# Leftover expert groups of 32 tokens, as four narrow fp32 products side by side inside the last large group's first layer

## The chip, the cores and the metric

The kernel runs on one core of one Trainium2 chip. The metric is device time in microseconds (us) of one execution. Three runs of the kernel before gave 670.18, 671.89 and 675.13 us; the median is 671.89 us.

## The reference, cut to what matters

Three layers follow each other. Attention with hash buckets (2 batches, 8 heads, 768 positions, 64 wide) gives 1536 rows of 512. A gated product without experts (`w1`, `w2`, `w3`, `w_out`) turns them into `x`, again 1536 x 512. A mixture of 8 experts ends the kernel, and the change is in it:

```python
def _moe2_ref(x, modality_id, w_gate, modality_bias, w1, w2):
    logits = x @ w_gate + modality_bias[modality_id]
    e_idx = np.argmax(logits, axis=1)
    ...                                   # probs, gate_w: the softmax weight of the chosen expert
    for e in range(E):
        mask = e_idx == e
        if not mask.any():
            continue
        h = np.maximum(x[mask] @ w1[e], 0.0)               # 512 -> 1024
        out[mask] = gate_w[mask, None] * (h @ w2[e])       # 1024 -> 512
    return out
```

Each token goes to one expert alone. With the inputs that the runs use, the argmax of the reference picks two experts only, one for 786 tokens and one for 750.

## The kernel before, in words

**Groups.** The tokens of one expert are cut into large groups of G = 256. What is left over (the count modulo 256) is another large group if it is more than 128, and otherwise a *leftover group* of 128 places (`half_group`, name "H"). For 786 tokens that is three large groups and 18 tokens in a leftover group, for 750 tokens three large groups (256, 256, 238). The program holds NFULL = 6 large groups and one leftover group in straight code (`static`), in that order; any further ones run in a loop at the end (`tc.For_i`), which runs no turn when there are none. Counts, thresholds (`cs[:, 16:28]`) and places (a column of 128 places per half of a large group, one column per leftover group, NCOL columns in all) are computed on the chip by VectorE (DVE), and the list of tokens of each column comes from 12 small products on TensorE (PE), `pv`.

**Products.** A large group is computed in three terms: each 32-bit operand is split into a rounded high part and the low rest (type fp32r), and high x high, high x low and low x high are summed (`TERMS`). `stage1` computes the first layer: for each of 8 blocks `f` of 128 hidden units, 12 products (4 chunks of the 512 inputs, 3 terms) of 128x128 weights with 256 tokens, then ScalarE (ACT) takes the ReLU as the high part and DVE the low part. `stage2` computes the second layer: for each of two halves of 128 tokens 24 products with 512 columns, then `put` scales by the gate and GpSimd (POOL) scatters the rows to `out`. A leftover group does the same with tokens as the stationary side: 24 products of 512 columns, 8 transposes, 24 products of 512 columns.

**Weights.** Each group loads its expert's two weight matrices anew, as 8 units of 512 KB (`load_raw`, issued by SyncE, SP, into a ring of 4 buffers). `split_raw` splits a unit: ACT copies the high part, DVE subtracts for the low part. The order is a list: `seq` gives the units in the order of the groups, `split_next` takes the next one, and calls `more_loads` for the load that may now use the buffer that has come free. `hook1` and `hook2` call `split_next` at fixed blocks of `stage1` and `stage2`, 8 times in a group, so that group j's hooks split the units of group j+1. `hook2` also issues the gathers (`gather`, POOL) of the group after next and the transposes (`trans`, PE) of the next one.

**Full 32-bit products.** Where both operands are plain fp32 (not fp32r) a product leaves two records in the trace. Four such products with a stationary side of 32 columns stand side by side (`tile_position=(0, 32*k)`, each writing its own 32 partitions of one PSUM tile) in several places of this kernel; two of them matter here. `logit_mm` (L708) has four of 384 columns, and `w34_gate` (L583) four of 128 columns:

```python
PE.matmul(lg_t[ch][k:k + 32, :], wgp[:, f, :], gf_t[ch, f4][:, f % 4, :], ..., tile_position=(0, k))       # L708
PE.matmul(pg[32 * c:32 * c + 32, :], wgs[:, c, :], wT[:, c, :], ..., tile_position=(0, 32 * c))            # L583
```

PSUM tiles: tag `ab` has 4 buffers, `t` has 2, `aw0` and `aw1` one each. The program's order on each engine is the order in which the code issues.

Of the kernel before, what the change touches and what calls it, by code (L numbers as in the profile page):

```python
# [20 lines left out]
P = 128  # L21
# [7 lines left out]
NFULL, MAXF, MAXH = 6, 9, 8  # L29
NCOL = 2 * MAXF + MAXH  # L30
# [43 lines left out]
def consts_array(proj):  # L74
# [17 lines left out]
    c[:, 16:28] = float(P) * np.arange(12)  # L92
# [78 lines left out]
def body(tc, qT, kT, vP, w1d, w2d, w3d, wod, mod, wgate, mbias, e1, e2, cst, out):  # L171
# [1006 lines left out]
    for i in range(2):  # L1178
        xg_t["F", 0, i] = r_xg([P, DM])
        POOL.memset(xg_t["F", 0, i], 0.0)  # L1180
    static = [("F", j) for j in range(NFULL)] + [("H", 0)]
    eregs = {
        (t, j): nc.values_load(
            egi[0:1, MAXF * (t == "H") + j:MAXF * (t == "H") + j + 1], engines=SPE, min_val=0, max_val=E - 1
# [5 lines left out]
    seq = [(j, m, k) for j in static for m in range(2) for k in range(4)]  # L1190
    lq = list(seq)
# [6 lines left out]
    def load_raw(j, m, k, e):  # L1198
        raw = r_er([P, 1024])
        SP.dma_start(raw if m == 0 else raw.rearrange("p (c f) -> p c f", c=2), unit_src(m, k, e))  # L1200
        eraw[j, m, k] = raw
# [90 lines left out]
    def cols(t, j):  # L1292
        if j[0] == "H":
            return [t[:, 2 * MAXF + j[1]:2 * MAXF + j[1] + 1]]
        return [t[:, 2 * j[1] + i:2 * j[1] + i + 1] for i in range(2)]

    def gather(j, idx, rows=NT):
        for i, ix in enumerate(idx):
            if (*j, i) not in xg_t:
                xg_t[*j, i] = r_xg([P, DM])  # L1300
            POOL.indirect_dma_start(
                out=xg_t[*j, i], out_offset=None, in_=x2d[0:rows, :],
# [62 lines left out]
    for span in gspan:  # L1365
        mem.give(span)

    r_eu.grow(2, 4 * 2 * 4096)
    r_h = ring("h", 2 * 8 * G, 2)
    r_o = ring("o", DM, 3)  # L1370
    r_hn = ring("hn", DF, 1)

    def trans(j):
        n = G if j[0] == "F" else P
        x = r_ex([P, 2, 4, n], F32R)
        for i in range(n // P):
# [34 lines left out]
    def stage2(j, gcol, scol, hook=None):  # L1411
        h = h_t.pop(j)
        w = wu.pop((j, 1)).rearrange("p x (c n) -> p x c n", c=8)
        for i in range(2):
# [7 lines left out]
            put(o, gcol[i], scol[i])  # L1422

    def put(o, gate_col, row_col, n=DM):
        ot = r_o([P, DM])
        ACT.activation(ot[:, 0:n], o[:, 0:n], AF.Copy, scale=gate_col)  # L1426
        if n < DM:
            DVE.tensor_scalar(ot[:, n:], o[:, n:], gate_col, None, ALU.mult)  # L1428
        POOL.indirect_dma_start(  # L1429
# [4 lines left out]
    def half_group(j, gcol, scol, hook=None):  # L1434
        hook = hook or (lambda n: None)
        x = x2_t.pop(j)
        w = wu.pop((j, 0)).rearrange("p x (c n) -> p x c n", c=4)
        hn = r_hn([P, DF])
        h = r_h([P, 2, 8, P], F32R)

        def htrans(n):
            t = ps("t", [P, 4, P], f"ht{j[0]}{j[1]}{n}")
            for c in range(4):
                PE.transpose(t[:, c, :], hn[:, n * 512 + c * P:n * 512 + c * P + P], ident)
            sl = slice(4 * n, 4 * n + 4)
            ACT.copy(h[:, 0, sl, :], t)
            DVE.tensor_sub(h[:, 1, sl, :], t, h[:, 0, sl, :].bitcast(F32))

        for n in range(2):
            o = ps("aw"[n], [P, 512], f"e1{j[0]}{j[1]}{n}")  # L1450
            for c in range(4):
                for i, (st, mv) in enumerate(TERMS):
                    PE.matmul(
                        o, x[:, st, c, :], w[:, mv, c, n * 512:n * 512 + 512],
                        start=(c == 0 and i == 0), stop=(c == 3 and i == 2),
                    )
                if n == 1 and c == 1:
                    htrans(0)
                hook(4 * n + c)
            ACT.activation(hn[:, n * 512:n * 512 + 512], o, AF.Relu)  # L1460
        w = wu.pop((j, 1)).rearrange("p x (c n) -> p x c n", c=8)
        o = ps("ab", [P, DM], f"e2{j[0]}{j[1]}")
        for f in range(8):
            for k, (st, mv) in enumerate(TERMS):
                PE.matmul(o, h[:, st, f, :], w[:, mv, f, :], start=(f == 0 and k == 0), stop=(f == 7 and k == 2))
            if f == 1:
                htrans(1)
            hook(8 + f)
        put(o, gcol[0], scol[0], DM // 2)
# [104 lines left out]
```

## Time and profile before

| | |
|---|---|
| three runs | 670.18, 671.89, 675.13 us |
| the profiled execution, its own time | 671.4 us |
| its span in the trace | 669.2 us |
| PE busy in the span | 640.7 us (96%) |
| DVE, ACT, POOL busy | 384.4, 318.5, 320.2 us |
| six large groups on PE | from 509.45 to 649.47 us of the span |
| the leftover group on PE, after them | from 649.31 to 661.34 us |
| from the last product to the end of the span | 7.9 us |

The times of the trace are microseconds from the start of the span. The profiled execution's own time is 2.2 us more than its span, and 0.5 us under the median of the runs.

### The profile page before, as it was taken

The page shows a single profiled execution, that of the slowest core. Times are in us where ns is not written, and L with a number is a line of the kernel's source. Part 1 is how long each engine was busy: PE and PEld are TensorE (multiplying, and loading weights), DVE is VectorE, ACT ScalarE, POOL GpSimd, SP SyncE. Part 2 cuts the span into 40 slices and gives each one's busy share as a digit, 9 for nine tenths or more (in the row PEclk, how much of TensorE's full clock was granted, in tenths as well). Part 3 has the DMA queues.
Part 4 walks back from the last instruction along what each step waited for, and adds up shares of the span by engine and source line. Part 5 has one row for each costly group of instructions (what it writes and reads, how often), then busy time and mean ns, then how long its engine had stood idle before and what let it go on. Part 6 is the DMA issues. An engine that isn't in the chain of part 4 may idle for free. (4 is left out here: it accounts for less than half of the span.)

```text
span 669.2 us, 10109 instructions
## 1 busy us (share of the span) xinstructions
PE 640.7 (96%) x3640; PEld 505.6 (76%) x3640; DVE 384.4 (57%) x573; ACT 318.5 (48%) x510; POOL 320.2 (48%) x291
## 2 busy tenths in 40 slices
PE   6998999999999998999999999999999999999995
PEld 2544666666666665687998988999889899889984
DVE  6798777667786999833531311211566775575551
ACT  7367575666556655753421220321134665565551
POOL 7598988686869777766341340421104222201110
PEclk9999999999999999999999999999999999999999
DMA  7747482654647474312302001000046896765630
GB/s 227 245 139 171 158 251 90 180 186 127 221 122 217 129 235 137 120 48 80 123 6 66 24 0 48 1 0 17 17 157 235 309 300 227 237 226 189 215 121 9
DMA packets 40662, 93.86 MB, mean 140 GB/s; under 512 B 6544, under 2 KB 11008, under 8 KB 40608
## 3 DMA queue, kind: packets, MB, share of 16 engines
q1 hardware_dynamic: 38528, 86.62, 41.9%
q0 software_dynamic: 2080, 6.56, 2.8%
q8 instruction: 30, 0.49, 0.3%
q14 instruction: 24, 0.20, 0.1%
HBM read 72.98 MB, written 12.94 MB: 128 GB/s over the span
## 5 line engine op out<-in xcount | busy, mean ns | idle before, releaser
L685 PE MATMUL ab<-x,w 128*128 128x384 f32 x512 | 135.3, 339 | 0.6 <-ACT ss L412 0.6
L385 POOL TENSOR_TENSOR acc<-acc,pt 128x770 f32<-128x770 f32 x64 | 119.9, 1873 | 21.6 <-ACT pt L380 19.9
L355 DVE TENSOR_REDUCE nm<-m 128x1 f32<-128x768 f32 x96 | 91.4, 955 | 49.6 <-PE m L347 49.2
L380 ACT ACTIVATE pt<-s 128x768 f32<-128x768 f32 x96 | 77.9, 811 | 72.0 <-PE s L379 69.8
L685 PEld LDWEIGHTS ab<-x,w 128*128 128x128 f32 x512 | 93.5, 188 | 5.8 <-issue 4.4
L379 PE MATMUL s<-q,k 128*128 128x384 f32 (+1 forms) x384 | 91.0, 359 | 4.0 <-ACT pt L380 3.8
L379 PEld LDWEIGHTS s<-q,k 128*128 128x128 f32 (+1 forms) x384 | 63.6, 189 | 38.7 <-issue 16.2
L697 POOL TENSOR_TENSOR g<-gf,g 128x384 fp32r<-128x384 f32 x32 | 32.9, 1029 | 119.5 <-ACT g L696 116.0
L685 PE MATMUL ab<-xlo,w 128*128 128x384 f32 x256 | 86.4, 338 | 0.0
L1217 DVE TENSOR_TENSOR eu<-er,eu 128x1024 fp32r<-128x1024 f32 x56 | 68.4, 1242 | 24.1 <-ACT eu L1216 22.6
L393 PE MATMUL a<-pt,v 128*64 128x385 f32 x384 | 74.5, 502 | 0.0
L1429 POOL DMA_INDIRECT out<-o,sidx x13 | 13.7, 1050 | 118.0 <-ACT o L1426 102.0
L1400 PEld LDWEIGHTS e1F<-ex,eu 128*128 128x128 f32 x576 | 69.2, 189 | 0.4
L1400 PE MATMUL e1F<-ex,eu 128*128 128x256 f32 x576 | 69.4, 281 | 0.0
L1419 PE MATMUL e2F<-eu,h 128*128 128x512 f32 x288 | 68.9, 395 | 0.0
L695 DVE TENSOR_TENSOR gf<-asb,ab 128x384 f32<-128x384 f32 x32 | 17.7, 553 | 84.0 <-PE ab L685 83.4
L1216 ACT CAST eu<-er 128x1024 fp32r<-128x1024 f32 x56 | 57.5, 1048 | 9.2 <-DMA er<-e 7.7
L1419 PEld LDWEIGHTS e2F<-eu,h 128*128 128x128 f32 x288 | 53.2, 188 | 11.4 <-DVE h L1406 0.3
L347 PE MATMUL m<-k,q 78*128 78x384 f32 x192 | 52.4, 355 | 5.2 <-DVE nm L355 2.7
L1024 PE MATMUL x2p<-w,g 128*128 128x512 f32 x240 | 57.4, 396 | 0.0
L1024 PEld LDWEIGHTS x2p<-w,g 128*128 128x128 f32 x240 | 44.8, 188 | 10.9 <-issue 0.6
L600 PE MATMUL w<-wo,w 128*128 128x512 f32 x192 | 49.0, 393 | 0.4 <-POOL w L495 0.4
(208 smaller groups left out, 863.0 us busy)
## 6 DMA issues: line engine op xcount, KB each, us to landing
er<-e SPq DMA_DIRECT2D x56, 512.0 KB
cr<-w3d SPq DMA_DIRECT2D x16, 512.0 KB
cr<-wod SPq DMA_DIRECT2D x8, 512.0 KB
cr<-w1d SPq DMA_DIRECT2D x8, 512.0 KB
wfd<-cT SPq DMA_DIRECT2D x16, 256.0 KB
cr<-w2d SPq DMA_DIRECT2D x8, 512.0 KB
st<-wfd SPq DMA_DIRECT2D x16, 256.0 KB
raw<-kT SPq DMA_DIRECT2D x8, 384.0 KB
```

What stands on the lines that cost most here:

```text
L347: PE.matmul(s[:, half, 0:HS], q[0:KROWS[hd], 0, qt * P:qt * P + P], k[0:KROWS[hd], 0, half * HS:half * HS + HS], start=True, stop=True,)
L355: DVE.tensor_reduce(nm[:, at:at + 1], s[:, :, 0:HS], AX.XY, ALU.max, negate=True)
L379: PE.matmul(s[:, hd, 0:HS], k[0:n, i, c * P:c * P + P], q[0:n, i, cl], start=(i == 0), stop=(i == 1))
L380: ACT.activation(pts[j % NP][:, :, 0:HS], s[:, :, 0:HS], AF.Exp, scale=SCALE)
L385: POOL.tensor_add(acc, pts[(j - 1) % NP] if c == 1 else acc, pts[j % NP])
L393: PE.matmul(a_t[p, half][64 * hd:64 * hd + 64, :], v[:, c, 64 * hd:64 * hd + 64], pts[j % NP][:, hd, :], start=(c == 0), stop=(c == QT - 1 ...
L685: PE.matmul(t, w12[j][:, st, c, fs], x[mv][:, c, :], start=(c == 0 and i == 0), stop=(c == 3 and i == 2))
L1024: PE.matmul(st["ps"], g_t[ch, f // 4][:, a, f % 4, i * P:i * P + P], w34[b][:, f, :], start=(f == 0 and k == 0), stop=(f == 7 and k == 2),)
L1216: ACT.copy(t[:, 0, sl], raw)
L1217: low = lambda: DVE.tensor_sub(t[:, 1, sl], raw, t[:, 0, sl].bitcast(F32))
L1400: PE.matmul(o[f], w[:, st, c, fs], x[:, mv, c, :], start=(c == 0 and i == 0), stop=(done and c == 3 and i == terms[-1]),)
L1419: PE.matmul(o, h[:, st, f, sl], w[:, mv, f, :], start=(f == 0 and k == 0), stop=(f == 7 and k == 2))
```

## The change: what it does, and the diff

A leftover group holds 32 places in place of 128; more than 32 tokens left over now make a large group. The one static leftover group is computed by `tiny_group` in four steps, which `hook1` issues after the blocks f = 0, 1, 2 and 3 of the last large group's `stage1`. Its products are full 32-bit ones of the loaded weights, without a split: the 32 tokens are the stationary side, and four products write four strips of 32 partitions. In the first layer a strip is a quarter of the 1024 hidden units (256 columns), in the second a quarter of the 512 outputs (128 columns). Its 8 weight units have buffers of their own (`tw`), and their loads stand one by one in the list after every fourth load of the large groups, from the 20th to the 48th. The hidden layer's buffer `h` of the large groups is one in place of two, and the last large group's last `put` is shared between ACT and DVE, as the leftover group's was.

```diff
-NFULL, MAXF, MAXH = 6, 9, 8
-NCOL = 2 * MAXF + MAXH
+NFULL, MAXF, MAXT = 6, 12, 8
+NCOL = 2 * MAXF + MAXT
+TINY_N = 32
...
-    c[:, 16:28] = float(P) * np.arange(12)
+    c[:, 16:28] = (G * np.arange(6)[:, None] + TINY_N * np.arange(2)[None, :]).reshape(12)
...
-    static = [("F", j) for j in range(NFULL)] + [("H", 0)]
+    static = [("F", j) for j in range(NFULL)] + [("T", 0)]
...
-    seq = [(j, m, k) for j in static for m in range(2) for k in range(4)]
-    lq = list(seq)
+    seq = [(j, m, k) for j in static[:NFULL] for m in range(2) for k in range(4)]
+    lq = []
+    for n, item in enumerate(seq):
+        lq.append(item)
+        if n >= 16 and n % 4 == 3:
+            lq.append((static[NFULL], (n - 19) // 16, (n - 19) // 4 % 4))
+    tw = []
...
-        raw = r_er([P, 1024])
+        if j[0] == "T":
+            raw = tw[m][k]
+        else:
+            raw = r_er([P, 1024])
...
                 load_raw(j, m, k, eregs[j])
+                while lq and lq[0][0][0] == "T":
+                    j, m, k = lq.pop(0)
+                    load_raw(j, m, k, eregs[j])
...
+    for n in ("lastx", "lastoh"):
+        rings[n].close()
...
-    r_h = ring("h", 2 * 8 * G, 2)
+    r_h = ring("h", 2 * 8 * G, 1)
     r_o = ring("o", DM, 3)
-    r_hn = ring("hn", DF, 1)
+    r_tx = ring("tx", 4 * TINY_N, 1)
+    r_hn = ring("hn", DF // 4, 1)
+    r_hT = ring("hT", DF // 4, 1)
+    tw += [[one(f"tw{m}{k}", [P, 1024]) for k in range(4)] for m in range(2)]
...
-            put(o, gcol[i], scol[i])
+            put(o, gcol[i], scol[i], DM // 2 if end and i else DM)
...
-    def half_group(j, gcol, scol, hook=None):
...
+    def tiny_group(j, gcol, scol):
+        n, st = TINY_N, {}
+
+        def transposed():
+            xg = xg_t.pop((*j, 0))
+            t = ps("t", [P, 4, n], f"et{j[0]}{j[1]}")
             for c in range(4):
+                PE.transpose(t[:, c, :], xg[0:n, c * P:c * P + P], ident[0:n, 0:n])
+            st["x"] = r_tx([P, 4, n])
+            ACT.copy(st["x"], t)
+
+        def layer1():
+            o = ps("t", [P, DF // 4], f"e1{j[0]}{j[1]}")
             for c in range(4):
+                for k in range(4):
+                    w = k * (DF // 4)
                     PE.matmul(
+                        o[n * k:n * k + n, :], st["x"][:, c, :], tw[0][c][:, w:w + DF // 4],
+                        start=(c == 0), stop=(c == 3), tile_position=(0, n * k),
                     )
+            st["h"] = r_hn([P, DF // 4])
+            ACT.activation(st["h"], o, AF.Relu)
+
+        def turned():
+            t = ps("t", [P, 2, P], f"ht{j[0]}{j[1]}")
+            for b in range(2):
+                PE.transpose(t[:, b, :], st["h"][:, b * P:b * P + P], ident)
+            st["hT"] = r_hT([P, 2, P])
+            ACT.copy(st["hT"], t)
+
+        def layer2():
+            o = ps("t", [P, P], f"e2{j[0]}{j[1]}")
+            for f in range(8):
+                k, b = divmod(f, 2)
+                for q in range(4):
+                    w = b * DM + q * P
+                    PE.matmul(
+                        o[n * q:n * q + n, :], st["hT"][:, b, n * k:n * k + n], tw[1][k][:, w:w + P],
+                        start=(f == 0), stop=(f == 7), tile_position=(0, n * q),
+                    )
+            raw, ot = r_o([P, DM]), r_o([P, DM])
+            for q in range(4):
+                DVE.tensor_copy(raw[0:n, q * P:q * P + P], o[n * q:n * q + n, :])
+            DVE.tensor_scalar(ot[0:n, :], raw[0:n, :], gcol[0], None, ALU.mult)
+            scatter(ot[0:n, :], scol[0])
+
+        return [transposed, layer1, turned, layer2]
 
     gather(static[1], cols(gidx, static[1]))
-    for n, j in enumerate(static):
+    tiny = tiny_group(static[NFULL], cols(inv[:, 1, :], static[NFULL]), cols(sidx, static[NFULL]))
+    for n, j in enumerate(static[:NFULL]):
         def hook1(f):
             if f % 2 == 1 or n == 0:
                 split_next()
+            if n == NFULL - 1 and f < 4:
+                tiny[f]()
...
```

The loop at the end is changed in the same way and is left out here.

On PE the end of the program reads as follows before; `e1F` and `e2F` are the two layers of the last large group, `etH`, `e1H`, `htH` and `e2H` the transposes and layers of the leftover group, with the output's shape and the number of products behind.

```order
L1400 MATMUL e1F_5980<-ex_5783,eu_5658 128x256 x12
L1419 MATMUL e2F_5999<-eu_5772,h_5861 128x512 x12
L1380 MATMUL etH_6016<-ident_70,xg_5798 128x128 x4
L1419 MATMUL e2F_5999<-eu_5772,h_5861 128x512 x12
L1419 MATMUL e2F_6042<-eu_5772,h_5861 128x512 x24
L1453 MATMUL e1H_6078<-eu_5892,ex_6015 128x512 x12
L1453 MATMUL e1H_6092<-eu_5892,ex_6015 128x512 x6
L1444 MATMUL htH_6099<-ident_70,hn_6076 128x128 x4
L1453 MATMUL e1H_6092<-eu_5892,ex_6015 128x512 x6
L1465 MATMUL e2H_6113<-eu_6006,h_6077 128x512 x6
L1444 MATMUL htH_6120<-ident_70,hn_6076 128x128 x4
L1465 MATMUL e2H_6113<-eu_6006,h_6077 128x512 x18
```

With the change the last large group's first layer is on PE (its blocks f = 0 to 4 are shown, with lines of the changed file; `etT`, `e1T`, `htT`, `e2T` are the steps of the leftover group):

```order
L1417 MATMUL e1F_5870<-ex_5797,eu_5673 128x256 x12
L1461 MATMUL etT_5885<-ident_70,xg_5812 128x32 x4
L1417 MATMUL e1F_5892<-ex_5797,eu_5673 128x256 x12
L1470 MATMUL e1T_5907<-tw_397_4650,tx_5890 32x256 x4
L1470 MATMUL e1T_5907<-tw_398_4651,tx_5890 32x256 x4
L1470 MATMUL e1T_5907<-tw_399_4652,tx_5890 32x256 x4
L1470 MATMUL e1T_5907<-tw_400_4653,tx_5890 32x256 x4
L1417 MATMUL e1F_5926<-ex_5797,eu_5673 128x256 x12
L1480 MATMUL htT_5941<-ident_70,hn_5924 128x128 x2
L1417 MATMUL e1F_5946<-ex_5797,eu_5673 128x256 x12
L1490 MATMUL e2T_5961<-tw_401_4654,hT_5944 32x128 x8
...
L1417 MATMUL e1F_6004<-ex_5797,eu_5673 128x256 x12
```

Three more rows of `e2T`, 8 products each, stand where the dots are. After block f = 7 come the 48 products of `e2F`, and nothing behind them.

On ACT the same stretch has, with the change, the ReLUs of the large group's blocks and the leftover group's copies between them; the four weight casts that stood there before are gone.

```order
L1422 ACTIVATE h_5869<-e1F_5870 128x256
L1463 COPY tx_5890<-etT_5885 128x128
L1422 ACTIVATE h_5869<-e1F_5892 128x256
L1475 ACTIVATE hn_5924<-e1T_5907 128x256
L1422 ACTIVATE h_5869<-e1F_5926 128x256
L1482 COPY hT_5944<-htT_5941 128x256
L1422 ACTIVATE h_5869<-e1F_5946 128x256
```

Each copy now stands right behind the ReLU of the block that PE computed just before the step.

## Rows read from the trace of the kernel before

**Rows 1.** The page: busy time by engine, and PE and its clock in 40 slices.
```profile
PE 640.7 (96%) x3640; PEld 505.6 (76%) x3640; DVE 384.4 (57%) x573; ACT 318.5 (48%) x510; POOL 320.2 (48%) x291
PE   6998999999999998999999999999999999999995
PEclk9999999999999999999999999999999999999999
```

**Rows 2.** Busy time by stretch, one per large group, then leftover group and tail.
```profile
core 0: us, PE busy (x) PEld busy (x) DVE busy (x) ACT busy (x) POOL busy (x), PEclk, DMA share, GB/s
509.90:532.60 22.70, 22.70 (x148) 20.36 (x147) 15.62 (x22) 14.32 (x23) 4.78 (x4) 1.00 0.83 300
532.60:556.00 23.40, 23.40 (x154) 21.20 (x153) 17.27 (x21) 14.70 (x22) 6.74 (x5) 1.00 0.90 287
556.00:579.50 23.50, 23.50 (x155) 21.43 (x154) 14.04 (x18) 13.06 (x20) 4.09 (x4) 1.00 0.71 229
...
626.60:649.50 22.90, 22.90 (x150) 20.88 (x149) 13.44 (x17) 12.56 (x19) 1.96 (x2) 1.00 0.47 147
649.50:661.40 11.90, 11.85 (x56) 9.43 (x55) 1.38 (x2) 3.06 (x5) 0.98 (x1) 1.00 0.05 21
661.40:669.30 7.90, 0.00 (x0) 0.00 (x0) 0.48 (x1) 0.47 (x1) 0.98 (x1) 0.83 0.03 8
```

**Rows 3.** Who waited for whom from 475 us on: total us, times, longest.
```profile
ACT eu L1216 <- DMA er<-e: 7.7, 7, 1.9
...
PE xb L1340 <- DMA xg<-x2d,gidx: 0.9, 1, 0.9
```

**Rows 4.** Timeline of PE, last large group: start us, length us, instructions merged.
```profile
626.58 11.47 PE L1400 MATMUL e1F<-ex,eu 128*128 128x256 f32 x96
637.88 2.93 PE L1419 MATMUL e2F<-eu,h 128*128 128x512 f32 x12
640.65 0.60 PE L1380 MATMUL etH<-ident,xg 128*128 128x128 f32 x4
641.01 8.46 PE L1419 MATMUL e2F<-eu,h 128*128 128x512 f32 x36
```

**Rows 5.** Timeline of the leftover group and the tail (some engines left out).
```profile
649.31 4.25 PE L1453 MATMUL e1H<-eu,ex 128*128 128x512 f32 x18
...
653.40 0.60 PE L1444 MATMUL htH<-ident,hn 128*128 128x128 f32 x4
...
653.75 1.62 PE L1453 MATMUL e1H<-eu,ex 128*128 128x512 f32 x6
...
656.96 4.38 PE L1465 MATMUL e2H<-eu,h 128*128 128x512 f32 x18
...
661.43 0.47 ACT L1426 ACTIVATE o<-e2H,inv 128x256 f32<-128x256 f32 x1 [3.60 <-PEq L1495]
661.94 0.48 DVE L1428 TENSOR_SCALAR o<-e2H,inv 128x256 f32<-128x256 f32 x1 [3.39 <-ACT o L1426]
662.70 0.98 POOL L1429 DMA_INDIRECT out<-o,sidx  x1 [11.20 <-DVE o L1428]
```

**Rows 6.** The scatters' line: shortest, median, longest in ns.
```profile
L1429 POOL DMA_INDIRECT out<-o,sidx x13: 977/993/1704, 532.8 to 662.7; - x13
```

**Rows 7.** Timeline of PE at four narrow full products of 384 columns, L708.
```profile
462.86 0.85 PE L708 MATMUL lg<-gf,wgp 128*32 128x384 f32 x8
463.65 0.44 PE L685 MATMUL ab<-x,w 128*128 128x384 f32 x1
```

**Rows 8.** Timeline of PE around four narrow full products of 128 columns, L583.
```profile
99.22 0.43 PE L583 MATMUL pg<-wT,wgs 128*32 128x128 f32 x8
99.58 0.97 PE L379 MATMUL s<-q,k 78*128 78x384 f32 x4
```

**Rows 9.** The same kind as rows 7 with its neighbours before and behind.
```profile
472.09 0.86 PE L1024 MATMUL x2p<-w,g 128*128 128x512 f32 x3
472.88 0.93 PE L708 MATMUL lg<-gf,wgp 128*32 128x384 f32 x8
473.74 1.20 PE L1024 MATMUL x2p<-w,g 128*128 128x512 f32 x4
474.77 0.49 PE L722 MATMUL lt<-ident,ls 128*128 128x128 f32 x3
```

**Rows 10.** Groups by line and shape: busy us, mean ns | idle before, by what.
```profile
L1405 ACT ACTIVATE h<-e1F 128x256 fp32r<-128x256 f32 x48 | 18.5, 384 | 26.8 <-PE e1F L1400 24.3 <-issue 1.0
L586 ACT COPY wT<-pg 128x128 f32<-128x128 f32 x8 | 2.1, 267 | 5.2 <-PE pg L583 5.2
```

**Rows 11.** SP's queue from 475 us on: what held its next load.
```profile
SPq L1200 <- DVE h L1406: 70.7, 23, 6.8
SPq L1200 <- DVE eu L1217: 38.9, 25, 2.3
```

**Rows 12.** Waits from 510 to 535 us, the first large group.
```profile
ACT eu L1216 <- DMA er<-e: 5.0, 5, 1.8
```

**Rows 13.** Groups by line: widest of the table operations that get more columns.
```profile
L1267 DVE TENSOR_TENSOR rr<-ohh,cs 128x312 f32<-128x312 f32 x1 | 0.5, 486 | 0.0
L1268 DVE TENSOR_TENSOR rr<-ohh,gate 128x312 f32<-128x312 f32 x1 | 0.5, 475 | 0.0
```

**Rows 14.** Single records of L708: shortest, median, longest in ns.
```profile
L708 PE MATMUL lg<-gf,wgp x64: 486/498/510, 316.1 to 473.3; 128*32 128x384 f32 x64
```

More of the change, by code (lines that the diff above doesn't have):

```diff
@@ L1409, in stage1, with stage2 @@
         h_t[j] = h
-    def stage2(j, gcol, scol, hook=None):
+    def stage2(j, gcol, scol, hook=None, end=False):
         h = h_t.pop(j)
@@ L1428, in put, with scatter @@
             DVE.tensor_scalar(ot[:, n:], o[:, n:], gate_col, None, ALU.mult)
+        scatter(ot, row_col)
+    def scatter(ot, row_col):
         POOL.indirect_dma_start(
@@ L1461, in half_group @@
[L1461 to L1469, printed above, removed]
+                        o[n * k:n * k + n, :], st["x"][:, c, :], tw[0][c][:, w:w + DF // 4],
@@ L1479, in hook2 @@
                 split_next()
-            if i == 3 and n + 1 < len(static):
+            if i == 3 and n + 1 < NFULL:
                 trans(static[n + 1])
-                if n + 2 < len(static):
-                    gather(static[n + 2], cols(gidx, static[n + 2]))
-        if j[0] == "F":
-            stage1(j, hook1, 0 if n else 2)
-            stage2(j, cols(inv[:, 1, :], j), cols(sidx, j), hook2)
-        else:
-            half_group(j, cols(inv[:, 1, :], j), cols(sidx, j))
+                gather(static[n + 2], cols(gidx, static[n + 2]))
+        stage1(j, hook1, 0 if n else 2)
+        stage2(j, cols(inv[:, 1, :], j), cols(sidx, j), hook2, n == NFULL - 1)
     lidx = [one(f"lidx{i}", [P, 2], I32) for i in range(2)]
@@ L1500, in body @@
             nc.values_load(eni[0:1, i:i + 1], min_val=a, max_val=b)
-            for i, (a, b) in enumerate(((NFULL, MAXF), (1, MAXH)))
+            for i, (a, b) in enumerate(((NFULL, MAXF), (1, MAXT)))
         ]
-        for kind, a in (("F", NFULL), ("H", 1)):
-            with tc.For_i(a, ends[kind == "H"], 1) as i:
-                j, nt = (kind, "L"), 2 if kind == "F" else 1
+        for kind, a in (("F", NFULL), ("T", 1)):
+            with tc.For_i(a, ends[kind == "T"], 1) as i:
+                j, nt, np = (kind, "L"), 2 if kind == "F" else 1, P if kind == "F" else TINY_N
                 er = nc.values_load(
@@ L1513, in body @@
                         load_raw(j, m, k, er)
-                        split_raw(j, m, k)
-                gi_, si_, gt_ = ([t[:, x:x + 1] for x in range(nt)] for t in (*lidx, lgt))
+                        if nt == 2:
+                            split_raw(j, m, k)
+                gi_, si_, gt_ = ([t[0:np, x:x + 1] for x in range(nt)] for t in (*lidx, lgt))
                 gather(j, gi_)
-                trans(j)
                 if nt == 2:
+                    trans(j)
                     stage1(j)
@@ L1521, in body @@
                 else:
-                    half_group(j, gt_, si_)
+                    for step in tiny_group(j, gt_, si_):
+                        step()
     ms.__exit__(None, None, None)
```

36 lines of the change are left out of this document (8 added, 28 removed).

## The prediction

> **What bounds the kernel now.** I first read the page's busy times and slices: PE is busy for 640.7 of 669.2 us and has its full clock in every slice; the other engines are at 57% or less [rows 1]. The chain of waits that ended last begins only at the last product, because an engine that never idles ends every such chain; so I went on to the stretches, one for each large group. PE is busy in all of each (23.40 of 23.40, 22.90 of 22.90) and in the 11.9 us of the leftover group behind them; then come 7.9 us in which PE does nothing [rows 2]. In the list of waits from 475 us on, PE has one of note, 0.9 us for a gather before the first large group [rows 3]. So in this part of the program a microsecond less on PE is a microsecond less in all, as long as nothing else becomes late, and DMA, ACT and DVE are read only for that. The timeline then gives the pieces [rows 4, 5]: the last large group's last product ends at 641.01 + 8.46 = 649.47, the leftover group's at 656.96 + 4.38 = 661.34, and from there run a half copy on ACT, the other half on DVE, the scatter and the program's end.
>
> **What is removed.** The leftover group's own time on PE, 661.34 - 649.47 = 11.87 us (48 products of 512 columns and 8 transposes), and its four transposes inside the last large group, 641.01 - 640.65 = 0.36 us [rows 4, 5]. Together 12.23 us. The 8 casts on ACT and 8 subtractions on DVE that split its weights go too; I price them at nothing, since PE waited for neither.
>
> **What stays.** With the change the last product is the last large group's, and its `put` is shared between ACT and DVE as the leftover group's was. So the same 7.9 us follow [rows 2, 5]. The scatter writes more rows, which I price at nothing: POOL took 0.98 us for the leftover group's 18 tokens, and the median of all 13 scatters, most of them of 128 rows, is 0.99 [rows 6].
>
> **What is added on PE.** Four steps between blocks of the last large group's first layer.
>
> First the narrow full products. The trace has two such sets of four. One of 384 columns takes 463.65 - 462.86 = 0.79 us from its start to the next product's [rows 7]; one of 128 columns 99.58 - 99.22 = 0.36 us [rows 8]. Each set has eight records, two a product. The difference, 0.43 us for 256 columns, gives 1.68 ns a column: 0.215 us for a set of 128 columns, 0.43 us for one of 256, and a fixed 0.145 us in both. The neighbours pay too: three products stand before the set from 472.09 to 472.88, 0.79 us, where at the stream's pace (12 in 640.65 - 637.88 = 2.77 us, so 0.231 us each) they would take 0.69, and four behind it take 474.77 - 473.74 = 1.03 in place of 0.92 [rows 4, 9]. That is 0.21 us for each change to narrow products and back.
>
> The first layer has 4 sets of 256 columns: 4 x 0.43 = 1.72, with the fixed part once 1.87, with the change of kind 2.08 us. If each set pays the fixed part, 2.51. The second layer has 8 sets of 128 columns: 1.72 + 0.145 + 0.21 = 2.08, or with the fixed part in each set 3.09. I take 2.1 and 2.3, near the lower ends: the fixed part stands where the set ends and another kind of product follows, which happens once in each step; a little is added in the second layer, whose records are so short that anything between them shows.
>
> Then the transposes. Four of 128 columns took 0.36 us in the same stream [rows 4]. The new four have 32 tokens on 32 partitions; no row shows a transpose of so few. At least 0.36, and with a change of kind 0.57; I take 0.5. The two of the hidden layer are half of 653.75 - 653.40 = 0.35 us [rows 5]: 0.18, or 0.39 with a change; I take 0.2.
>
> Sum: 0.5 + 2.1 + 2.3 + 0.2 = 5.1 us (4.7 to 6.6).
>
> **What lies beside it.** Each step needs the one before through ACT. Cover is one block of the large group, 11.47 / 8 = 1.43 us [rows 4]. Against it stand 0.25 us by which the last transpose's record outlasts the start of the next product (0.60 - 0.35, [rows 5]), the block's ReLU of 0.38 that is ahead in ACT's queue, and a copy of 0.27 or 0.38 [rows 10]: 0.9 to 1.0 us. It fits, and no cast is left in ACT's queue there. Were the cover gone, three hand-offs would cost up to 1.0 each. The four small DVE copies and the multiply stand ahead of the block f = 4's subtraction; the tag `ab` has four buffers, so PE may run on for some blocks. The one `h` buffer costs nothing: its next writer reads a product that stands behind its last reader on PE.
>
> **Loads.** The 8 units of 0.524 MB move forward and stand in SP's queue among the large groups' loads. SP's queue is paced by buffers coming free, 48 times after the first eight [rows 11]; a `tw` load waits for no buffer and goes at once. Three fall into the stretch 532.60 to 556.00, which is at 287 GB/s and 0.90 of the DMA engines already [rows 2]: 1.57 MB in 23.4 us, 67 GB/s more than there is room for at the 300 GB/s of the stretch before. So some casts will wait, each for up to one unit (0.524 MB at 300 GB/s, 1.75 us). The stretch before shows what that costs: ACT waited 5 times and 5.0 us for loads there [rows 12], and PE was busy for 22.70 of 22.70 us [rows 2]. I price it at nothing, because a unit is split a second layer (649.47 - 637.88, some 11 us) before PE needs it [rows 4].
>
> The tables get 32 columns in place of 26: the widest operations, 0.49 us each [rows 13], grow by less than a quarter, some 0.3 us in all, beside products that PE has in its queue. Nothing.
>
> **Sum.** 12.23 - 5.1 = 7.1 us less, 671.4 - 7.1 = **664.3 us**; with the bounds of the added steps (4.7 to 6.6) 663.9 to 665.8. The profiled execution lies 0.5 us under the median of the runs, so the median after may as well be 664.8.
>
> **The rivals.**
>
> *Strict order.* Each strip's second record needs the strip for itself after the first. If PE starts records only in program order, the next strip's first record waits behind it, and a set takes four turns in place of two: 32 turns of 0.1075 and 16 of 0.215 us, 3.44 us a layer in place of 1.72, so 3.4 us more: 667.7. Against it: eight records of 0.498 us [rows 14] passed in 0.79 us; four turns at 0.32 us (384 columns at 1.68 ns, two turns a set) would be 1.29. But no row shows more than one set in a line. Chance 0.07. The Trainium skill, "TensorE: Matmul & The Clock Gate", section "The mechanism" in Part 3, states just this order: products begin and end in the order of the program, without reordering. By that rule it would be the forecast; the trace differs, with 0.79 us for the set.
>
> *One strip after another* (slower than before). The strips share one PSUM bank and differ in weights; if in a long accumulation they take turns, all 96 records follow one another: 32 x 0.215 + 64 x 0.1075 = 13.8 us in place of 3.4, which is 674.6; with the fixed 0.145 us for each of them too, another 13.6, 688. It decides at (12.23 - 0.7 - 0.4) / 96 = 0.116 us a record. The single sets speak against it. Chance 0.03.
>
> *A late load or a late hand-off.* PE is held once for one unit, 666.0, or for the three of the full stretch, 664.3 + 5.2 = 669.5. For it: the DMA at 0.90. Against it: the stretch before. Chance 0.08, mostly near 666.
>
> *It is not one leftover group.* If an expert had 33 to 128 tokens left over, the loop at the end would run a seventh large group: 23 us on PE behind at least 14 us for its eight units at 300 GB/s, over 700 us. The inputs say 18 tokens. Chance 0.02.
>
> **How the numbers follow.** Forecast 0.78, the four rivals 0.20, others 0.02. A change of under 1% can't be told from none here; 1% of 671.89 is 6.7 us, so the line is at 665.2, inside my forecast's own range of 663.9 to 665.8. About seven tenths of the forecast lie beyond it: 0.55 faster. Strict order, late loads and the rest of the forecast are within 1%: 0.41. Slower by over 1% needs strips in turn with their fixed parts, the loop, or something unseen: 0.04. The range runs from 662.9, one us under the lower bound since runs of one kernel differ by as much, to 668.0, which takes in strict order and one late unit.
>
> **What would show it.** PE's timeline of the last large group: `e1F` with four insertions; `e1T` from its start to the next `e1F` about 2.0 us and `e2T` about 2.2 (3.8 each by strict order, 7 or more in turn), no PE idle before them, then 48 products of `e2F` and 7.9 us. ACT's waits for loads may rise to 10 us between 532 and 556 with PE still full. The prediction is wrong if PE waits on ACT or a load inside the last two groups, if the steps take over 6.6 us together, or if the tail has grown.

## The result, and the profile after

The changed kernel takes 663.17 us in the median of 6 runs (662.62 to 665.12); the kernel before, run beside it, took 671.5 (670.18 to 675.13). The ratio is 0.9881, with an interval of 0.9865 to 0.9898. A second comparison on another chip gave 663.3 against 670.89, ratio 0.9882 (0.9865 to 0.9898). The profiled execution took 663.34 us, with a span of 661.5: 7.7 us less than the 669.2 of before.

First the page of the changed kernel: PE's busy time, and PE and its clock in 40 slices.

```profile
PE 633.1 (96%) x3682; PEld 498.8 (75%) x3682; DVE 374.9 (57%) x567; ACT 308.4 (47%) x499; POOL 318.0 (48%) x291
PE   6998999999999998999999999999999999999995
PEclk9999999999999999999999999999999999999998
```

PE is busy for 7.6 us less than in [rows 1], which is nearly the whole difference. It is as full as before, and its granted clock has the digit 9 in all slices but the last, which holds the tail. The stretches of the changed kernel say the same (columns as in [rows 2]; the last stretch here runs from the end of the group before into the last large group's first layer):

```profile
509.90:532.60 22.70, 22.70 (x149) 20.60 (x148) 16.89 (x23) 15.55 (x24) 5.67 (x5) 1.00 0.84 295
532.60:556.00 23.40, 23.40 (x153) 21.25 (x152) 15.87 (x20) 13.45 (x21) 4.53 (x5) 1.00 0.88 317
556.00:579.50 23.50, 23.50 (x156) 21.42 (x155) 14.04 (x18) 13.05 (x20) 4.09 (x4) 1.00 0.77 267
618.00:641.00 23.00, 23.00 (x225) 19.80 (x224) 9.17 (x17) 8.12 (x16) 2.89 (x3) 1.00 0.20 72
```

PE's first number equals the stretch's length in each, and the granted clock is 1.00: the four steps are in the last row (225 products), and PE waits for nothing there. The moved loads show in the second row, 317 GB/s in place of 287.

PE's timeline of the last large group, with the four steps `etT`, `e1T`, `htT` and `e2T`, answers to [rows 4]. Columns are start, length and products merged; a line's length runs into the next line's, so a step's price is the distance between starts.

```profile
626.27 1.58 PE L1417 MATMUL e1F<-ex,eu 128*128 128x256 f32 x12
627.78 0.43 PE L1461 MATMUL etT<-ident,xg 32*128 32x32 f32 x4
628.14 1.68 PE L1417 MATMUL e1F<-ex,eu 128*128 128x256 f32 x12
629.75 1.93 PE L1470 MATMUL e1T<-tw,tx 128*32 128x256 f32 x32
631.61 1.64 PE L1417 MATMUL e1F<-ex,eu 128*128 128x256 f32 x12
633.09 0.38 PE L1480 MATMUL htT<-ident,hn 128*128 128x128 f32 x2
633.22 1.66 PE L1417 MATMUL e1F<-ex,eu 128*128 128x256 f32 x12
634.81 1.95 PE L1490 MATMUL e2T<-tw,hT 128*32 128x128 f32 x64
636.69 5.71 PE L1417 MATMUL e1F<-ex,eu 128*128 128x256 f32 x48
642.24 11.04 PE L1436 MATMUL e2F<-eu,h 128*128 128x512 f32 x48
```

The steps take 628.14 - 627.78 = 0.36, 1.86, 0.13 and 1.88 us, 4.23 together. The group's first layer lasts 642.24 - 626.27 = 15.97 us where it lasted 637.88 - 626.58 = 11.30 [rows 4]: 4.67 more, so 0.44 us lie with the neighbours of the four insertions, 0.11 for each on average. The second layer takes 11.04 where it took 649.47 - 637.88 = 11.59 [rows 4]. The last product ends at 653.28, before at 661.34.

The other engines at these steps and in the tail, which answers to [rows 5] (the brackets are idle time before, and what ended it):

```profile
628.25 0.27 ACT L1463 COPY tx<-etT 128x128 f32<-128x128 f32 x1
631.75 0.38 ACT L1475 ACTIVATE hn<-e1T 128x256 f32<-128x256 f32 x1 [1.51 <-PE e1T L1470]
636.83 1.18 DVE L1496 COPY o<-e2T 32x128 f32<-32x128 f32 x4 [1.07 <-PE e2T L1490]
638.04 0.47 DVE L1497 TENSOR_SCALAR o<-o,inv 32x512 f32<-32x512 f32 x1
653.32 0.47 ACT L1443 ACTIVATE o<-e2F,inv 128x256 f32<-128x256 f32 x1 [4.70 <-PE e2F L1436]
653.83 0.48 DVE L1445 TENSOR_SCALAR o<-e2F,inv 128x256 f32<-128x256 f32 x1 [10.55 <-ACT o L1443]
654.59 0.98 POOL L1449 DMA_INDIRECT out<-o,sidx  x1 [4.71 <-DVE o L1445]
```

ACT's copies are done at 628.52 and 632.13, about a microsecond before the next step starts on PE (629.75, 633.09). From the last product to the scatter it is the same 1.3 us as before, but from there to the end 6.87 in place of 6.47.

Who waited for whom from 475 us on (total us, times, longest), against [rows 3]:

```profile
ACT eu L1229 <- DMA er<-e: 6.8, 7, 2.0
PE xb L1353 <- DMA xg<-x2d,gidx: 0.7, 1, 0.7
```

ACT's waits for loads are no more in all than before (7.7 us in 7, the longest 1.9), and PE's one wait is for the gather before the first large group, as before. All 7 fall before 532.6 us; in the stretch from there to 556 us, which moves more bytes than before, ACT waits for no load.

**The sum by pieces.** From the last group's start to its last product it is 653.28 - 626.27 = 27.01 us; before, with the leftover group behind it, 661.34 - 626.58 = 34.76. That is 7.75 us less: 11.87 of the leftover group and 0.55 in the second layer, against 4.67 for the steps. The group starts 0.31 us earlier, of which the shorter wait for the gather explains 0.2; the tail is 0.36 longer; the span 7.7 shorter.

### The profile page after: what moved, and what is told of

The parts are those of the page before. It is cut to its first block, busy times and chain, and to the rows that moved or that the text cites. A ratio compares the mean times of both kernels' runs of the same rounds, so it can differ in the third digit from the quotient of the medians.

```text
span 661.5 us, 10163 instructions
## 1 busy us (share of the span) xinstructions
PE 633.1 (96%) x3682; PEld 498.8 (75%) x3682; DVE 374.9 (57%) x567; ACT 308.4 (47%) x499; POOL 318.0 (48%) x291
## 4 chain that ended last, share of the span: by engine, by line
PE 82%; DVE 6%; POOL 3%; ACT 3%; DMA 2%; issue 2%; SPq 0%; POOLq 0%; DVEq 0%; ACTq 0%
PE ab L686 21%; PE e1F L1417 10%; PE e2F L1436 10%; PE x2p L1025 8%; PE s L380 8%; PE a L394 7%; PE w L601 6%; PE m L348 4%; DVE nm L356 2%; POOL acc L386 1%; ACT pt L381 1%; DMA x2d<-xo 1%; PE lg L709 1%; DVE u L519 1%; PE n L409 1%
## 5 line engine op out<-in xcount | busy, mean ns | idle before, releaser
L1230 DVE TENSOR_TENSOR eu<-er,eu 128x1024 fp32r<-128x1024 f32 x48 | 58.6, 1244 | 18.9 <-ACT eu L1229 18.4
L1229 ACT CAST eu<-er 128x1024 fp32r<-128x1024 f32 x48 | 49.4, 1048 | 6.9 <-DMA er<-e 6.8
```

Of the source, the lines that this page charges most:

```text
L1230: low = lambda: DVE.tensor_sub(t[:, 1, sl], raw, t[:, 0, sl].bitcast(F32))
```

## The experiments

Two theories stood from the start. By the first, the time is PE's: the leftover work costs what its products take on PE, four strips abreast, and loads, hand-offs and buffers are free. Against it stood that the loads or hand-offs cost something too and the products less, or that the strips run abreast only in part. Where spans are compared below, one thing has to be taken out first: PE's waits for gathers, near 503 and 525 us, change from profile to profile (0.71 us in all in the changed kernel, 3.1 in one further below) and shift everything behind. So pieces are measured from the last large group's first product on.

### What the four steps cost

**Without the steps** (`e1_no_steps`): the loads stay.

```diff
-            if n == NFULL - 1 and f < 4:
-                tiny[f]()
```

> The four steps of the leftover group are left out (its 18 tokens get no output); its loads and its gather stay. Theory (the steps cost what they take on PE, and nothing else of them is on the path): the first layer of the last large group falls from 15.97 us (626.27 to 642.24) back to about 11.4, the span from 661.5 to 657.0, 4.5 less. Rival (the steps cost more than their own time, by waits on ACT or by the loads): the span falls by 6 or more. Rival (they are hidden beside other work): by less than 3.

658.65 us, span 656.9. PE in the last large group:

```profile
626.64 11.47 PE L1417 MATMUL e1F<-ex,eu 128*128 128x256 f32 x96
637.95 11.09 PE L1436 MATMUL e2F<-eu,h 128*128 128x512 f32 x48
```

From the group's first product to its last it is 22.40 us (637.95 + 11.09 - 626.64). The changed kernel has 27.01, so the four steps cost 4.61 us, all of it on PE.

**Without the loads too** (`e2_no_loads`).

```diff
-        if n >= 16 and n % 4 == 3:
-            lq.append((static[NFULL], (n - 19) // 16, (n - 19) // 4 % 4))
...
-            if n == NFULL - 1 and f < 4:
-                tiny[f]()
```

> As the one without steps, and the eight loads of the leftover group's weights are left out too. Theory (the added loads are off the path): the span is that of the kernel without steps, 657.0, to 0.5; the DMA engines' share in 532.6 to 556 falls from 0.88 to about 0.75. Rival (the moved loads cost PE time): 1.5 to 5 less than without steps alone.

658.34 us, 0.3 less than with the loads; PE's waits for gathers were 0.9 us shorter in this profile (0.30 us at 503 us, against 0.83 and 0.35 at 503 and 525), which more than covers it. All eight loads are issued between 535.7 and 618.0 us (in the run with them), from the second large group's start to before the last one's, so the way from the one's first product to the other's shows their price. The second large group's first layer with the loads, then both groups' without them:

```profile
533.26 11.55 PE L1417 MATMUL e1F<-ex,eu 128*128 128x256 f32 x96
```

```profile
532.64 11.55 PE L1415 MATMUL e1F<-ex,eu 128*128 128x256 f32 x96
...
626.05 11.47 PE L1415 MATMUL e1F<-ex,eu 128*128 128x256 f32 x96
```

It is 626.64 - 533.26 = 93.38 us with the loads and 626.05 - 532.64 = 93.41 without. The stretch in which the first two of the loads fall, and in which the third is issued at its very end (555.87 us), in the kernel with the loads and then in this one:

```profile
532.60:556.00 23.40, 23.40 (x154) 21.26 (x153) 16.62 (x21) 14.07 (x22) 5.92 (x5) 1.00 0.89 316
```

```profile
532.60:556.00 23.40, 23.40 (x153) 21.20 (x153) 15.95 (x20) 13.46 (x21) 4.66 (x5) 1.00 0.81 281
```

The DMA moves 281 GB/s in place of 316, and PE is busy for 23.40 of 23.40 us in both. The loads lie off the path.

**The kernel before without its leftover group** (`e9_before_no_leftover`): transposes, products and output left out, loads and splits kept.

```diff
-        else:
-            half_group(j, cols(inv[:, 1, :], j), cols(sidx, j))
...
-                trans(static[n + 1])
+                if n + 1 < NFULL:
+                    trans(static[n + 1])
```

> The kernel before with the leftover group's transposes, products and output left out (its 18 tokens get no output); its loads, casts and subtractions stay. Theory (all of its PE time was on the path, 11.87 + 0.36 us): the span falls from 669.2 to about 657.0, which is that of the changed kernel without its steps (656.9); so nothing else in the change (loads, one buffer for h, wider tables, four casts fewer) gains or costs 0.5 us. Rival (a part of the gain comes from the casts and loads that the change removed or moved): 658.5 or more.

656.99 us, span 655.1. PE in the last large group:

```profile
625.76 11.47 PE L1400 MATMUL e1F<-ex,eu 128*128 128x256 f32 x96
637.07 11.09 PE L1419 MATMUL e2F<-eu,h 128*128 128x512 f32 x48
```

Again 22.40 us: stripped of leftover work, both kernels spend the same. So before the leftover group cost PE 34.76 - 22.40 = 12.36 us, and the steps in its place 4.61; the difference, 7.75, is the change. Its span is 1.8 us under that of the changed kernel without steps because its last group starts 0.88 earlier (PE waits for no gather in this profile, and for 1.18 us in the other), and its tail is 0.9 shorter, of which more below. Not run was a leftover group of 32 places with its operands split as before, so what the full 32-bit products are worth apart from the narrow group stays open.

### Do the strips run abreast?

**One strip of the four** (`e3_one_strip`): only the first quarter of the hidden units and of the outputs is computed, the rest of the PSUM tile is set to zero on DVE.

```diff
+            st["o1"] = ps("t", [P, DF // 4], f"e1{j[0]}{j[1]}")
+            DVE.memset(st["o1"], 0.0)
...
-                for k in range(4):
+                for k in range(1):
...
-                for q in range(4):
+                for q in range(1):
```

> Only the first of the four strips is computed in both layers (three quarters of the leftover group's products are left out; its 18 rows come out incomplete). Theory (the strips run beside each other, each at its own pace): the two layers take as long as with four strips, 1.86 and 1.88 us, to 0.1, and the span stays at 661.5 to 0.5. Rival (four strips share something, a port or the start of records): the layers fall towards a half, 0.9 to 1.4 us each, and the span by 1 to 2.

663.49 us, as much as with four strips. PE's timeline:

```profile
629.91 1.91 PE L1472 MATMUL e1T<-tw,tx 128*32 128x256 f32 x8
631.76 1.63 PE L1417 MATMUL e1F<-ex,eu 128*128 128x256 f32 x12
...
634.91 1.93 PE L1494 MATMUL e2T<-tw,hT 128*32 128x128 f32 x16
636.77 5.93 PE L1417 MATMUL e1F<-ex,eu 128*128 128x256 f32 x48
```

8 records take 1.85 us and 16 take 1.86; four times as many took 1.86 and 1.88. Three of the four strips cost nothing. The time is that of the records within one strip, which follow each other every 0.216 us in the first layer, every 0.109 in the second. These records add onto the same sums, but that this sets their pace is not shown: the transposes `htH` of the kernel before, also plain fp32 and 128 columns long, add onto nothing and follow each other every 0.109 us too.

**Strip by strip** (`e4_strip_by_strip`): the same products, each strip's in a row.

```diff
-            for c in range(4):
-                for k in range(4):
+            for k in range(4):
+                for c in range(4):
...
-            for f in range(8):
-                k, b = divmod(f, 2)
-                for q in range(4):
+            for q in range(4):
+                for f in range(8):
+                    k, b = divmod(f, 2)
```

> The same products, but written strip by strip: all products of the first strip, then all of the second, and so on. Theory A (a strip starts its next record when it is free, however far back it stands in the program): no change, layers of 1.9 us each. Theory B (PE looks ahead over some records only): the first layer, 32 records, stays under 4 us and the second, 64 records, goes to 3 to 7. Rival C (records start only in the order of the program, and the measured order happens to suit it): 32 x 0.216 = 6.9 us and 64 x 0.109 = 7.0 us, the span 661.5 + 10.2 = 671.7, where the kernel before was.

670.06 us; the kernel before took 670.34 beside it. Nearly the whole gain is gone. PE's timeline:

```profile
629.80 4.59 PE L1470 MATMUL e1T<-tw,tx 128*32 128x256 f32 x32
634.32 1.63 PE L1417 MATMUL e1F<-ex,eu 128*128 128x256 f32 x12
...
637.47 5.96 PE L1490 MATMUL e2T<-tw,hT 128*32 128x128 f32 x64
643.36 5.93 PE L1417 MATMUL e1F<-ex,eu 128*128 128x256 f32 x48
```

The layers take 4.52 and 5.89 us in place of 1.86 and 1.88, 6.67 us more. From the last group's first product to its last it is 33.85 us, against 27.01 in the changed kernel and 34.76 before: 6.84 of the 7.75 us are lost. One strip behind the other would be four times 1.73 and four times 1.74, near 7 us each. Between the two lies what the single records of the first layer show. They don't name their strip; two rows of starts 0.216 us apart tell two strips from each other. Strip 0's records start at 629.799, 630.039, 630.255, 630.471 and 630.687, and strip 1's first at 630.693, before strip 0's last three. The third and fourth strips begin in the same way, at the fifth of eight records (631.586 behind 631.580, 632.479 behind 632.474), and in the second layer at the thirteenth of sixteen. So PE does pass records that wait for their strip, but in both layers only once no more than three of them are left. 8 + 3 x 4 = 20 rounds of 0.216 are 4.3 us, and 16 + 3 x 12 = 52 of 0.109 are 5.7. In the order of the change a strip's next record is never far behind, and all four start within 20 ns (629.748, 629.754, 629.761, 629.768 us).

### The hand-offs and the loads

**The steps at the end** (`e5_at_the_end`): issued behind the last group's second layer, where nothing covers them.

```diff
-            if n == NFULL - 1 and f < 4:
-                tiny[f]()
...
+    for step in tiny:
+        step()
```

> The four steps come after the last large group's second layer in place of between the blocks of its first. Theory (the blocks of 1.43 us cover three hand-offs through ACT, and the last copies on DVE): PE idles some 0.4 to 0.6 us at each of three hand-offs, and 1.7 us of DVE copies stand between the last product and the scatter in place of 1.0 us of put: the span goes from 661.5 to 664.0, 663.3 to 664.7. Rival (the place is worth nothing, PE only adds the products up): 661.0 to 661.8.

666.96 us, span 665.2. PE's timeline:

```profile
650.57 0.43 PE L1461 MATMUL etT<-ident,xg 32*128 32x32 f32 x4
651.41 1.93 PE L1470 MATMUL e1T<-tw,tx 128*32 128x256 f32 x32 [0.41 <-ACT tx L1463]
653.85 0.44 PE L1480 MATMUL htT<-ident,hn 128*128 128x128 f32 x2 [0.50 <-ACT hn L1475]
654.75 1.96 PE L1490 MATMUL e2T<-tw,hT 128*32 128x128 f32 x64 [0.46 <-ACT hT L1482]
```

The three hand-offs now show as idle time: 0.41 + 0.50 + 0.46 = 1.37 us. The last group starts 1.97 us later than in the changed kernel, 1.69 of it a wait for a gather at 526 us. Without that shift the span is 36.93 us from the group's start where the changed kernel has 35.19, 1.7 more: 1.4 in hand-offs, 0.3 behind the last product. The span is above both ranges on record (up to 664.7) only because of this shift; without it, it would be 663.2, at the lower end of what was expected with open hand-offs. So the blocks of the large group cover 1.4 us in all, about half of what I had allowed (up to 1.0 for each).

**All eight loads in a row** (`e7_loads_bunched`), behind the 20th load.

```diff
-        if n >= 16 and n % 4 == 3:
-            lq.append((static[NFULL], (n - 19) // 16, (n - 19) // 4 % 4))
+        if n == 19:
+            lq += [(static[NFULL], m, k) for m in range(2) for k in range(4)]
```

> All eight loads of the leftover group's weights (4.2 MB) stand behind the 20th load of the large groups, at about 535 us, in place of one after every fourth. Theory (ACT may wait for a load for a long time before PE does): ACT's waits for loads rise from 6.8 us to between 10 and 20, the 21st load's cast comes some 8 to 12 us late, PE loses 0 to 2 us, the span is 661.5 to 663.5. Rival (loads are near the path): each microsecond of lateness costs PE one, 5 to 12 us, 667 to 674.

666.07 us. ACT and PE where it is held up, ACT first:

```profile
555.86 1.05 ACT L1229 CAST eu<-er 128x1024 fp32r<-128x1024 f32 x1 [9.41 <-DMA er<-e]
556.81 1.07 ACT L1399 CAST ex<-etF 128x512 fp32r<-128x512 f32 x2
```

```profile
557.93 0.39 PE L1417 MATMUL e1F<-ex,eu 128*128 128x256 f32 x1 [0.81 <-ACT ex L1399]
559.41 11.46 PE L1417 MATMUL e1F<-ex,eu 128*128 128x256 f32 x95 [1.10 <-DVE ex L1400]
```

A cast waits 9.41 us for its load, and PE stands still for 0.81 + 1.10 = 1.9 us. From the second large group's first product to the last group's first it is 629.37 - 533.54 = 95.83 us, where the changed kernel has 626.27 - 532.75 = 93.52, so PE loses 2.3 us in all; the span, 664.3, lies between the two ranges on record. But PE doesn't wait for the weights that this cast makes: it waits for `ex`, the next group's transposed tokens, which stand behind the cast in ACT's queue. So a load may be late by some 9.41 - 2.3 = 7.1 us here before PE loses time; the longest wait in the changed kernel is 2.0.

### The tail

The longer tail raised the question whether the last `put`, shared between ACT and DVE, could be better. Three variants, timed beside the changed kernel:

> The changed kernel itself, as the measure for the two below: 663.2 us, 0.988 of the kernel before. From the last product's end to the last scatter's start 1.31 us, 3.40 us more until its rows have landed, 8.2 us in all to the span's end.

> The last put is a whole copy on ACT (0.69 us by the same line elsewhere) in place of 0.47 us on ACT and then 0.48 us on DVE, which waits for ACT. Theory: the time from the last product's end to the scatter's start falls from 1.31 to 1.0 us, the tail by 0.3, and the span to 661.2. Rival (the two halves help, since they overlap): 0.2 more.

> The last put whole on ACT, timed. Theory A (the shared put costs twice: 0.3 us in the hand-over from ACT to DVE and POOL, and 0.7 us in a scatter that lands later): 1.1 us less than the changed kernel, 662.1 us. Theory B (the later landing was chance, only the put counts): 0.3 us less, 662.9 us, with a landing of about 3.3 us.

> The last half of the last group's second layer is computed as two blocks of 256 columns, one after the other, and ACT reads the first while PE computes the second. Theory A: 48 products of 256 columns at half the time of 24 of 512, so nothing added on PE; behind the last product only a copy of 256 columns, 0.47 in place of 0.69 us, so 0.8 us to the scatter, a tail of 6.9 us, and 0.2 us less than with the put whole on ACT: 661.9 us. Theory B: the narrower products cost PE 0.2 us or more, or its reading beside PE holds PE up, and nothing is gained over that kernel.

> The last put whole on DVE. From the last product to the scatter about 1.2 us (a copy of 512 columns on DVE is estimated at twice its half's 0.48 us). Theory A (a scatter lands later when DVE wrote last): 3.1 to 3.4 us from the scatter's start to its landing, tail about 8. Theory B (a scatter lands later when two engines share the put): 2.6 to 2.7 us, tail about 7.3.

The edits are, for the whole `put` on ACT and (with ACT's part left out where n is 0) on DVE:

```diff
-            put(o, gcol[i], scol[i], DM // 2 if end and i else DM)
+            put(o, gcol[i], scol[i])                             # e6_put_on_act, e6_again
+            put(o, gcol[i], scol[i], 0 if end and i else DM)     # e10_put_on_dve
```

and for the last half of the last group in two blocks of columns:

```diff
+            if end and i:
+                ot = r_o([P, DM])
+                for b in range(2):
+                    cl = slice(b * 256, b * 256 + 256)
+                    o = ps("ab", [P, DM], f"e2{j[0]}{j[1]}{i}{b}")[:, 0:256]
...
+                                o, h[:, st, f, sl], w[:, mv, f, cl],
...
+                    ACT.activation(ot[:, cl], o, AF.Copy, scale=gcol[i])
+                scatter(ot, scol[i])
+                return
```

| kernel | runs, us | last product to scatter | scatter to landing | last product to end |
|---|---|---|---|---|
| before | 670.89 | 1.35 | 2.99 | 7.82 |
| the changed kernel, first profile | 663.17 | 1.31 | 3.40 | 8.18 |
| the same, second profile | 663.3 (662.65 to 664.54) | 1.31 | 3.21 | 7.99 |
| put on ACT, first profile | 662.03, one run beside 670.0 of before | 1.00 | 2.67 | 7.13 |
| put on ACT, second profile | 662.69 (662.13 to 665.49) | 1.00 | 3.15 | 7.62 |
| two blocks | 663.24 (661.95 to 663.52) | 0.79 | 3.21 | 7.47 |
| put on DVE | 663.76, one run | 1.07 | 3.03 | 7.57 |

The first profile of the put on ACT had made me believe that a shared put also delays the landing by 0.7 us. The second one withdraws that: the same kernel landed its rows 3.15 us after the scatter's start. Over all profiles the landing takes 2.6 to 3.5 us, by no rule that these runs show; the leftover rows before (18) were within that too. What does repeat is the way to the scatter: 1.00 us with ACT alone, against 1.31 shared. The last copy and the scatter with the put on ACT (second profile), and then with the put on DVE:

```profile
656.11 0.69 ACT L1443 ACTIVATE o<-e2F,inv 128x512 f32<-128x512 f32 x1 [4.70 <-PE e2F L1436]
657.08 0.98 POOL L1449 DMA_INDIRECT out<-o,sidx  x1 [4.40 <-ACTq L1525]
```

```profile
654.44 0.75 DVE L1446 TENSOR_SCALAR o<-e2F,inv 128x512 f32<-128x512 f32 x1 [10.04 <-PE e2F L1436]
655.47 0.97 POOL L1450 DMA_INDIRECT out<-o,sidx  x1 [4.47 <-DVEq L1526]
```

A whole put costs 0.69 or 0.75 us, where its halves took 0.47 and 0.48: sharing saves nothing here, since the halves run one after the other (DVE waits for ACT) and a half takes more than half of a whole. In time, put on ACT stands at 0.9873 of before (0.9857 to 0.9890) against 0.9882 (0.9865 to 0.9898): 0.6 us less in the medians, which can't be told from nothing here. The two blocks save another 0.21 us behind the last product and lose more on PE:

```profile
642.91 5.60 PE L1450 MATMUL e2F<-eu,h 128*128 128x512 f32 x24
648.35 5.91 PE L1440 MATMUL e2F<-eu,h 128*128 128x256 f32 x48
```

From the last group's first product to its last it is 27.32 us (648.35 + 5.91 - 626.94) against 27.01. No version beat the changed kernel by an amount that can be measured.

## Why the prediction was right, point by point

Forecast 664.3, measured 663.17; the mechanism held, and most terms were a little too dear. The measured time lies below the bounds of the added steps (663.9 to 665.8), and inside the range (662.9 to 668.0) only by the one microsecond that was taken off for the spread of the runs. Of the three signs of being wrong one did show: the tail has grown.

- **PE bounds this part of the program.** Held. Without the steps the last product comes 4.61 us sooner after the group's start, and the span falls by 4.6; without the leftover group the kernel before has its last product 12.36 us sooner, and its span falls by 14.1, the rest by gathers and the tail.
- **Removed, 12.23 us.** It was 11.87 + 0.55 = 12.42, or 12.36 by the run without the leftover group. The term for `etH` was read as 0.36 us, without the change of kind at its neighbours that I counted for every added set.
- **Added, 5.1 us.** It was 4.67, and 4.61 against the kernel without steps. The terms that failed: 0.21 us for each change to narrow products and back, read from a set among products of 512 columns [rows 9], was 0.11 on average; and the 0.2 us that I put on the second layer for its short records were nothing. The layers themselves are as worked out, 1.86 and 1.88 for 4 x 0.43 + 0.145 = 1.87. The transposes of 32 columns took 0.36, the lower bound, and 0.47 with their change of kind, where I took 0.5. The two of the hidden layer took 0.13, under the 0.18 that I read as half of four: they start 0.11 us apart, but the next product starts 0.03 us behind the last of them, in both sets.
- **Strict order** (667.7, chance 0.07). Refuted. Each strip's first record would have waited behind the second record of the strip before; the four start within 20 ns. The kernel before shows it in single records already: in the set of [rows 8] the four strips' first records start at 99.221 to 99.241 us, and the second ones from 99.355 on. I had judged the sets by their length alone. In strip-by-strip order, where the program leaves no doubt, strip 1's first record starts at 630.693 us, ahead of strip 0's last three (630.903 and later). The Trainium skill, "TensorE: Matmul & The Clock Gate", section "The mechanism" in Part 3, states that products start and end in program order, with none passing another; the trace of these 32-bit products differs. Yet the rival had half a point: the passing stops at about three waiting records, and with another loop order the kernel lost 6.84 of the 7.75 us that it had won. I hadn't asked what the order of the loops was worth.
- **One strip after another** (674.6 to 688, chance 0.03). Refuted for this order, by the run with one strip.
- **Loads at nothing.** Right, but for a partly wrong reason. I took 300 GB/s as all the room there is; the stretch from 532.60 to 556.00 moved 317, and no cast waited in it. Nor did three units fall into it: two did, and the third was issued as it ended (555.49 us). I gave some 11 us between a unit's split and its use. The path that closes first is another: the next group's transposed tokens stand behind the late cast in ACT's queue, and leave some 7 us.
- **Hand-offs at nothing.** Right; uncovered they cost 1.4 us in all.
- **The tail, the same 7.9 us.** Not quite, and its growth was a sign of being wrong by the prediction's own words: 8.2 and 8.0 in the two profiles, against 7.8. What failed is one of two terms: the scatter's rows, priced at nothing, or its landing, taken as fixed. The landing of the scatter was 3.40 and 3.21 us against 2.99. Whether its 128 rows in place of 18 are the cause stays open, since the landing spreads from 2.6 to 3.5 with the same rows, and the run without the steps, with the same put and rows, has a tail of 7.83.

Of the 1.1 us between the forecast and the measured median, 0.6 are these terms on PE (7.75 against 7.1); the earlier start's 0.3 and the longer tail's 0.4 cancel. Of the rest, 0.35 is that the profiled execution's own time is 1.9 us above its span here and was 2.2 before, and 0.2 that the median lies under the profiled execution; both are within the spread of the runs.

## What to carry to other kernels

When products use a narrow part of PE, put them side by side and go round the strips in turn: the records of one strip then set the time, and the other strips come free (1.85 us for one strip, 1.86 for four). Put short dependent steps between blocks of a longer independent product stream, so that their hand-offs to other engines cost nothing, and look in the queue of each such engine for what stands behind a late load. Compare pieces from a fixed point in the program, before spans: two profiles of one kernel (the put on ACT) have the last group's start at 626.10 and 629.07 us, 3.0 apart, and 2.5 of that are waits for gathers far ahead of the change.

## What the runs showed of the hardware

- Four narrow full 32-bit products of 32 stationary columns, in four strips, take the time of one: 1.85 us for 8 records of 256 columns in one strip, 1.86 for 32 in four.
- PE starts a record ahead of earlier ones that wait for their strip, but only with about three of those still ahead: strips follow each other at the fifth of 8 and the thirteenth of 16 records.
- A transpose of 32 rows into 32 columns comes every 0.06 to 0.08 us, four in 0.36 us with what surrounds them.
- From its start to its landing a last scatter takes 2.6 to 3.5 us; two profiles of one kernel differ by 0.5.
- The waits for the first gathers differ by 2.4 us between profiles of kernels that are the same there (0.71 us, and 1.13 + 0.23 + 1.73 = 3.09).
